# A two-layer cached-attention decode kernel, rewritten around one circular SBUF buffer: K half on TensorE and half on VectorE, contiguous K/V reads, layer 2 run backwards over the last unit kept

## The chip, the cores and the metric

The kernel runs on one core of one Trainium2 chip; the other cores are idle. The metric is the device time of one execution in microseconds (us), lower is better. Of the kernel before there are three timed runs, with a median of 2951.37 us (2937.76 to 2956.49), and one profiled execution, from which every other figure of the kernel before in this document comes.

## The reference

Two layers, each an attention over a cached K and V for one new token (batch 2, 32 heads, 16384 positions, head size 128) and a small mixer MLP. Everything is bf16. Both layers use the same K, V and weights.

```python
def _A_ref(x, k_cache, v_cache, wq, wo):          # x: (2, 1, 576)
    q = (lambda x, *d: x.transpose(*d))((x @ wq).reshape(B, Sq, H, Dh), 0, 2, 1, 3)   # wq: (576, 4096)
    scores = jnp.einsum("bhqd,bhkd->bhqk", q, k_cache) * (Dh ** -0.5)
    p = _softmax(scores, axis=-1)
    o = jnp.einsum("bhqk,bhkd->bhqd", p, v_cache)
    return (lambda x, *d: x.transpose(*d))(o, 0, 2, 1, 3).reshape(B, Sq, H * Dh) @ wo   # wo: (4096, 576)

def _B_ref(x, w1, w2, w3, w4):
    h = _gelu(_layernorm(x, axis=-1) @ w1)
    g0 = jnp.pad(h[:, :, 0*c:1*c], ((0, 0), (1, 0), (0, 0)))[:, :S, :]   # g1, g2, g3 alike, by 1 or 2
    ...
    hs = jnp.concatenate([g0, g1, g2, g3], axis=-1) @ w2
    x1 = x + hs
    h2 = _gelu(_layernorm(x1, axis=-1) @ w3) @ w4; return x1 + h2   # w3: (576, 4608), w4: (4608, 576)

x = x + _A_ref(_layernorm(x, axis=-1), A_k_cache, A_v_cache, A_wq, A_wo)
x = x + _B_ref(_layernorm(x, axis=-1), B_w1, B_w2, B_w3, B_w4)
x = x + _A_ref(_layernorm(x, axis=-1), A_k_cache, A_v_cache, A_wq, A_wo)
x = x + _B_ref(_layernorm(x, axis=-1), B_w1, B_w2, B_w3, B_w4)
```

The sequence has one position, so each shift moves all of h out and hs is a product of zeros with w2. A unit below is one (batch, head) pair: 64 a layer, each with 4.19 MB of K and 4.19 MB of V.

## The kernel before, in words

`Prog` collects closures for each engine, in the order in which they are added; every semaphore wait is written by hand. `attention_core` (L824 on) walks the 64 units of a layer. Each unit's K and V come in two halves of 2 MB (one tile of 128 partitions x 64 rows x 128, a run of 16 KB for each partition, with 32 KB from one partition's run to the next in HBM: `k_src`, `v_src`). K halves rotate through 4 buffers (`kbuf`), V halves through 5 (`vbuf`), weights through 5 slots (`wring`) with a plan of their own. All loads are issued by SP in one order (L1118 to L1126): K of unit u, then V of unit u-1. In front of a K load SP waits until the old half in that buffer has been used: `kfree_waits` waits for PE's transposes (`sem_kfree_pe`) and DVE's dots (`sem_kfree_dv`, which a one-element copy on DVE, L1044, counts up).

K needs its 128-element rows contracted with q. NCP = 6 of a unit's 16 chunks (a chunk is 8 blocks of 128 rows) go through PE: eight transposes into PSUM (L924), a copy to SBUF on ACT (L994, `ktsb`, 4 buffers), eight matmuls with q as the moving column (L949), 2 chunks behind. The other 10 chunks go through DVE (`dve_dots`): q is spread over the partitions with a diagonal and a matmul of ones (L1006, L962, L1015), then K times q in place (L1036) and a sum over each row (L1039): one pair of instructions for 2 chunks in the first half, one for 8 in the second.

The softmax of a unit: DVE takes the maximum over the two kinds of scores (L1052, L1057, L1063), POOL the maximum over the partitions with `partition_all_reduce` (L1072) and the scaling (L1075), ACT the two exponentials (L1086, L1090), and PE the 128 matmuls with V (L978). On ACT the exponentials stand in the same queue as the copies of the next unit's chunks.

Behind the last unit of a layer comes a chain of small steps: the denominators (POOL, L804 and L807), `wo_projection` over 32 heads (L537), the layernorms (`layernorm_T`, each with a POOL all-reduce), `z_projection` with w3 (L696), gelu, `w4_projection`, the product of w1 whose value is never used (`dead_h_projection`, L757), and the q projection of the next layer. Each matmul of these has a weight tile of 128 x 128 and two moving columns. The loads of w2, w3, w4, w1 and wq are issued at the layer's end, each when a slot of `wring` is free.

Of the kernel before, what the change touches and what calls it, by code (L numbers as in the profile page):

```python
# [8 lines left out]
ROP = bass.bass_isa.ReduceOp  # L9
# [6 lines left out]
class Prog:  # L16
    ENGS = ("sync", "scalar", "tensor", "vector", "gpsimd")

    def __init__(self):
        self.ops = {e: [] for e in self.ENGS}  # L20

    def add(self, eng, fn):
        self.ops[eng].append(fn)

    def emit(self, block):
        for e in self.ENGS:
            fns = self.ops[e]
            if not fns:
                continue

            def runner(eng, fns=fns):
                for fn in fns:
                    fn(eng)
            sect = {"sync": block.sync, "scalar": block.scalar, "tensor": block.tensor,
                    "vector": block.vector, "gpsimd": block.gpsimd}[e]
            sect(runner)


class KB:
    def __init__(self, nc, A_x, K, V, wq, wo, w1, w2, w3, w4, out,  # L40
                 NKB=5, NVB=4, NKT=5, NT=4, LEAD=2, NS=2, NP=2, NW=4, ACT_COPY_EVERY=3,
                 PV_AFTER=None, KV_WAIT_WQ=0, WENG="sync", WO_AT=(8, 16, 24, 32), NCP=None):
        self.nc = nc
        self.prog = Prog()
        self.A_x, self.K, self.V = A_x, K, V
        self.wq, self.wo, self.w1, self.w2, self.w3, self.w4 = wq, wo, w1, w2, w3, w4
        self.out = out
        B, Sq, D = A_x.shape
        Bk, H, S, Dh = K.shape
        assert Bk == B and Dh == 128 and Sq == 1  # L50
        self.B, self.D, self.H, self.S = B, D, H, S
        self.F = w3.shape[1]
        assert self.F % 128 == 0 and B <= 32
        assert tuple(wq.shape) == (D, H * 128) and tuple(wo.shape) == (H * 128, D)
        assert tuple(w1.shape) == (D, D) and tuple(w2.shape) == (D, D) and tuple(w4.shape) == (self.F, D)
        self.NL = 2
        self.U = B * H
        self.NB = S // 128
        self.CH = 8
        assert self.NB % self.CH == 0 and S % 128 == 0  # L60
        self.NC = self.NB // self.CH
        self.NPART = 2 if (self.NC % 2 == 0 and self.NC >= 2) else 1
        self.CP = self.NC // self.NPART
        self.BP = self.NB // self.NPART
        self.NCP = self.NC if NCP is None else NCP
        assert 1 <= self.NCP <= self.NC
        self.NKB, self.NVB, self.NKT, self.NT = NKB, NVB, NKT, NT
        self.LEAD, self.NS, self.NP, self.NW = min(LEAD, self.NCP), NS, NP, NW
        self.ACT_COPY_EVERY = ACT_COPY_EVERY
        self.PV_AFTER = PV_AFTER  # L70
        self.KV_WAIT_WQ = KV_WAIT_WQ
        self.WENG = WENG
        self.WO_AT = WO_AT
        self.KT = (D + 127) // 128
        self.klen = [min(128, D - 128 * t) for t in range(self.KT)]
        self.MT = self.F // 128
        self.scale = float(Dh) ** -0.5
        self.WCOLS = max(H * 128, self.F, self.KT * D, 512)
        self.W4G = max(1, min(self.MT, self.WCOLS // D))
        while self.MT % self.W4G:  # L80
            self.W4G -= 1
        self.WOG = max(1, min(H, self.WCOLS // D))
        while H % self.WOG:
            self.WOG -= 1
        assert self.NT == 4 and self.KT <= 5, "output tile groups use banks tps0..3 + mps"
# [1135 lines left out]
```

## Time and profile before

| what | value |
|---|---|
| median of the timed runs | 2951.37 us (2937.76 to 2956.49) |
| span of the profiled execution | 2954.2 us; nothing lies around it |
| read from HBM | 1116.51 MB, 378 GB/s over the span |
| DMA queue of SP | 96520 packets, 92.9% of 16 engines' span |
| DVE, PE, ACT, POOL busy | 79%, 47%, 28%, 3% |
| K and V loads | 512 tiles of 2 MB |
| granted TensorE clock | 0.521 on the mean |

The page lists busy times by engine, then the span in 40 slices with the busy share in tenths and the rate of the loads; the groups of instructions by line carry the mean time of one; the stretches ("windows") give the busy time of each engine, the granted clock, the DMA share and the rate between two times. A DMA share of 1.00 says that all 16 DMA engines had a packet in hand all the time; small excesses over 1 come from packets counted where they started.

### The profile page before, as it was taken

What the parts mean: (1) busy time and instruction counts of PE and PEld (TensorE: products, weight loads), DVE (VectorE), ACT (ScalarE), POOL (GpSimd) and SP (SyncE); (2) the same over time, 40 slices, a digit from 0 to 9 for tenths busy, and PEclk for the clock granted to TensorE, in tenths of its full rate; (3) what the DMA queues carried; (4) which work ended last, traced back from release to release, by engine and by line L of the source; (5) the groups of instructions that cost most, each with busy time, mean ns of one, the idle gap of its engine ahead of it and who ended that gap; (6) DMA issues with size and microseconds to landing.
All of it is one profiled execution on the core that took longest, in us unless ns stands there. A gap on an engine that the chain in (4) does not pass through costs nothing.

```text
span 2954.2 us, 67140 instructions
## 1 busy us (share of the span) xinstructions
PE 1389.2 (47%) x30282; PEld 1337.0 (45%) x30282; DVE 2325.3 (79%) x1554; ACT 841.6 (28%) x1304; POOL 92.8 (3%) x283
## 2 busy tenths in 40 slices
PE   3454544444544445444544444444454454544445
PEld 3444444444544445444544444444454444444445
DVE  5888888788788888888277887887888878888782
ACT  2322322322323223232122232232232322323221
POOL 0000000000000000000000000000000000000000
PEclk7555555555555555555555555555555555555555
DMA  9999999999999999999599999999999999999984
GB/s 393 411 400 398 393 393 378 379 386 403 386 391 386 398 389 387 393 371 395 193 410 401 398 383 397 388 376 395 385 398 394 386 388 394 380 393 390 380 361 154
DMA packets 96804, 1120.82 MB, mean 379 GB/s; under 512 B 8964, under 2 KB 28680, under 8 KB 28680
## 3 DMA queue, kind: packets, MB, share of 16 engines
q1 hardware_dynamic: 96520, 1116.54, 92.9%
q8 instruction: 238, 3.90, 0.5%
q14 instruction: 46, 0.38, 0.0%
HBM read 1116.51 MB, written 0.00 MB: 378 GB/s over the span
## 4 chain that ended last, share of the span: by engine, by line
issue 53%; PE 31%; ACT 6%; DVE 6%; POOL 3%; DMA 1%; POOLq 0%; ACTq 0%; SPq 0%; DVEq 0%
PE ops L978 14%; PE tps L924 11%; PE sps L949 4%; ACT ktsb L994 4%; ACT p_sb L1090 2%; POOL mall_sb L1072 2%; DVE s_dve L1039 1%; POOL bias_sb L1075 1%; DVE m_sb L1052 1%; DVE m_sb L1057 1%; DVE kbuf L1036 1%; DVE m_sb L1063 1%; ACT p_sb L1086 1%; PE tps L537 1%; DMA kbuf<-in_A_k_cache_dram 0%
## 5 line engine op out<-in xcount | busy, mean ns | idle before, releaser
L1039 DVE TENSOR_REDUCE s_dve<-kbuf 128x16 f32<-128x2048 bf16 (+1 forms) x256 | 1404.3, 5486 | 8.8
L949 PE MATMUL sps<-qt_sb,ktsb 128*128 128x1 bf16 x6144 | 302.2, 170 | 1321.9 <-ACT ktsb L994 1320.6
L949 PEld LDWEIGHTS sps<-qt_sb,ktsb 128*128 128x128 bf16 x6144 | 303.3, 114 | 1355.2 <-ACT ktsb L994 1353.7
L994 ACT ACTIVATE ktsb<-tps 128x1024 bf16<-128x1024 bf16 x768 | 741.3, 1023 | 424.7 <-PE tps L924 419.3
L924 PE MATMUL tps<-ident,kbuf 128*128 128x128 bf16 x6144 | 782.3, 309 | 13.5 <-DMA kbuf<-in_A_k_cache_dram 9.0
L1036 DVE TENSOR_TENSOR kbuf<-kbuf,qb_sb 128x2048 bf16<-128x2048 bf16 (+1 forms) x256 | 723.2, 2825 | 12.9 <-issue 1.3
L924 PEld LDWEIGHTS tps<-ident,kbuf 128*128 128x128 bf16 x6144 | 602.4, 140 | 15.1 <-DMA kbuf<-in_A_k_cache_dram 9.3
L1086 ACT ACTIVATE p_sb<-sps,bias_sb 128x48 bf16<-128x48 f32 x128 | 38.4, 300 | 1566.5 <-POOL bias_sb L1075 1566.5
L978 PE MATMUL ops<-p_sb,vbuf 128*128 128x1 bf16 x16384 | 456.0, 165 | 26.6 <-ACT p_sb L1086 19.7
L978 PEld LDWEIGHTS ops<-p_sb,vbuf 128*128 128x128 bf16 x16384 | 447.4, 104 | 26.8 <-ACT p_sb L1086 19.8
L1052 DVE TENSOR_REDUCE m_sb<-s_dve 128x1 f32<-128x80 f32 x128 | 30.2, 236 | 374.2 <-PE sps L949 373.9
L962 PE MATMUL mps<-diag_sb,ones_bf 128*128 128x128 bf16 x128 | 36.9, 289 | 136.4 <-DVE diag_sb L1006 136.4
L1072 POOL PARTITION_ALL_REDUCE mall_sb<-m_sb x128 | 50.3, 393 | 1282.6 <-DVE m_sb L1063 1238.5
L1075 POOL TENSOR_SCALAR bias_sb<-mall_sb 128x1 f32<-128x1 f32 x128 | 35.7, 279 | 1448.3 <-issue 1448.3
L962 PEld LDWEIGHTS mps<-diag_sb,ones_bf 128*128 128x128 bf16 x128 | 13.4, 105 | 146.7 <-DVE diag_sb L1006 146.7
L1015 DVE CAST qb_sb<-mps 128x128 bf16<-128x128 f32 x128 | 37.2, 291 | 53.9 <-PE mps L962 53.9
L1044 DVE CAST junk<-ident 128x1 f32<-128x1 bf16 x256 | 39.4, 154 | 27.1 <-DVE s_dve L1039 0.9
L1090 ACT ACTIVATE p_sb<-s_dve,bias_sb 128x80 bf16<-128x80 f32 x128 | 44.7, 349 | 0.0
L1006 DVE TENSOR_SCALAR diag_sb<-ident,qt_f 128x128 bf16<-128x128 bf16 x128 | 31.6, 247 | 0.1
L354 ACT ACTIVATE rstd<-var,epsb 128x2 f32<-128x2 f32 x8 | 2.4, 295 | 100.9 <-DVE var L347 100.9
L1057 DVE TENSOR_REDUCE m_sb<-sps 128x1 f32<-128x48 f32 x128 | 26.5, 207 | 4.5
L815 DVE RECIPROCAL rden_sb<-den_sb 128x64 f32<-128x64 f32 x2 | 1.1, 552 | 31.9 <-POOL den_sb L807 31.9
(91 smaller groups left out, 282.4 us busy)
## 6 DMA issues: line engine op xcount, KB each, us to landing
kbuf<-in_A_k_cache_dram SPq DMA_DIRECT2D x256, 2048.0 KB, 10.1
vbuf<-in_A_v_cache_dram SPq DMA_DIRECT2D x256, 2048.0 KB, 18.6
wring<-in_B_w_dram SPq DMA_DIRECT2D x12, 864.0 KB, 9.9
wring<-in_A_wo_dram SPq DMA_DIRECT2D x8, 1152.0 KB, 23.0
wring<-in_B_w_dram SPq DMA_DIRECT2D x8, 1152.0 KB, 6.8
wring<-in_A_wq_dram SPq DMA_DIRECT2D x8, 1024.0 KB, 9.8
wring<-in_B_w_dram SPq DMA_DIRECT2D x6, 576.0 KB, 8.6
wring<-in_A_wq_dram SPq DMA_DIRECT2D x2, 512.0 KB, 12.4
```

The lines of the kernel that those rows point to most:

```text
L924: ins = pe.transpose(self.tps[slot][:, i * 128:(i + 1) * 128], self.kbuf[kslot][:, jj, :], self.ident[:, :])
L949: ins = pe.matmul(self.sps[sb][:, j:j + 1], lhsT=self.ktsb[:, ks, i, :], rhs=self.qt_sb[:, gu:gu + 1], start=True, stop=True)
L978: ins = pe.matmul(self.ops_[:, gu:gu + 1], lhsT=self.vbuf[vslot][:, jj, :], rhs=self.p_sb[pb][:, j:j + 1], start=(j == 0), stop=(j == NB - 1))
L994: ins = eng.activation(out=self.ktsb[:, ks, :, :], in_=src, func=ACT.Copy)
L1036: dv.tensor_tensor(out=kap, in0=kap, in1=qb_bc, op=ALU.mult).then_inc(self.sems["sem_dotm"], 1)
L1039: dv.tensor_reduce(out=self.s_dve[ss][:, j0 - NBP:j1 - NBP], in_=kap, axis=AX.X, op=ALU.add).then_inc(self.sems["sem_dot"], 1)
L1052: i1 = dv.tensor_reduce(out=self.m2_sb[:, gu:gu + 1], in_=self.s_dve[sb][:, 0:NBD], axis=AX.X, op=ALU.max)
L1057: i2 = dv.tensor_reduce(out=self.m_sb[:, gu:gu + 1], in_=self.sps[sb][:, 0:NBP], axis=AX.X, op=ALU.max)
L1072: g_.partition_all_reduce(self.mall_sb[:, gu:gu + 1], self.m_sb[:, gu:gu + 1], channels=128, reduce_op=ROP.max).then_inc(self.sems["sem_po ...
L1075: g_.tensor_scalar(out=self.bias_sb[:, gu:gu + 1], in0=self.mall_sb[:, gu:gu + 1], scalar1=-scale, scalar2=None, op0=ALU.mult).then_inc(se ...
L1086: act.activation(out=self.p_sb[pb][:, 0:NBP], in_=self.sps[sb][:, 0:NBP], func=ACT.Exp, bias=self.bias_sb[:, gu:gu + 1], scale=scale, accu ...
L1090: act.activation(out=self.p_sb[pb][:, NBP:NB], in_=self.s_dve[sb][:, 0:NBD], func=ACT.Exp, bias=self.bias_sb[:, gu:gu + 1], scale=scale, a ...
```

## The change

The kernel is written anew; only the mathematics of a chunk stays. The parts are:

- **`Sched`** replaces the hand-written semaphores: every operation names what it reads and writes, and waits are worked out at build time. One counting semaphore an engine, 32 in turn for the DMAs.
- **`Ring`**: one SBUF tensor of 12 slots of 2 MB. All loads (K, V and weights) are queued in order of use and placed one behind another, wrapping at the end. `pump` runs at build time: a load is issued, on SP, as soon as the tiles that lie under its place have been released, and it waits for their last readers. A tile marked `keep` is stepped over.
- **Reads**: half h of a unit's K or V is now 16384/2 consecutive rows, so 2 MB in one piece: partition p holds 64 consecutive rows, and the next partition's run of 16 KB follows directly.
- **K half on PE, half on DVE**: half 0 (8 chunks) is transposed on PE and copied by ACT, half 1 (8 chunks) goes through DVE in pieces of one chunk, into two product buffers instead of in place.
- **Softmax**: the maximum over the partitions comes from an fp32 matmul with a scaled identity (`unit_max`) and a DVE reduction; POOL only makes constants. The query rows come from one matmul of a broadcast q column with the identity, copied by ACT.
- **Order**: the first two chunks of unit i are turned before `unit_max` of unit i-1; its exponentials stand behind the fifth copy on ACT; V of unit i-1 is weighed behind unit i's eight turns.
- **Output projection** in groups of 8 heads (`group_out`), four a layer; layernorm sums over partitions on PE; gelu through Exp, so that one ACT table serves everything.
- **Layer 2 backwards**: unit 63 is last in layer 1 and first in layer 2; its K and V (4 slots) stay in the ring. w2 is loaded once, w1 never.

The diff, cut to its core (the old functions stand above; `pump` belongs to `Ring`, all that follows to `Decode`; behind the loop of `plan` shown here w3 is queued in 5 tiles, w4 in 3, and in layer 1 wq in 5):

```diff
-    k = KB(nc, A_x, A_k_cache, A_v_cache, A_wq, A_wo, B_w1, B_w2, B_w3, B_w4, out, NKB=4, NVB=5, NW=5, NKT=4, NCP=6, ACT_COPY_EVERY=1)
-            return K[b, hh].rearrange("(p j) d -> p j d", p=128)[:, h * BP:(h + 1) * BP, :]
+    CH = 8
+    LEAD = 2
+    NKT = 3
+    NSLOT = 12
+    GH = 8
+    N_KEEP = 1
...
+    def pump(self):
+        while self.queue:
+            key, n, src, aligned = self.queue[0]
+            p = self._place(n, aligned)
+            if p is None:
+                return
+            under = [t for t in self.live if t["off"] < p + n and p < t["off"] + t["n"]]
+            if not all(t["done"] for t in under):
+                return
+            self.queue.pop(0)
+            deps = [o for t in under for o in self.s.readers(t["res"])]
...
+            self.s.dma(lambda e, src=src, view=view: src(e, view), w=[t["res"]], deps=deps)
+        def kv(src, u, h):
+            b, hh = u % B, u // B
+            ap = src[b, hh].rearrange("(t p j) d -> t p (j d)", t=2, p=128)[h]
+            return lambda e, v: e.dma_start(v, ap)
+        self.order = [list(range(self.U)), list(reversed(range(self.U)))]
...
+        want_wq(0)
+        for l in range(2):
...
+            for i, u in enumerate(order):
+                if u not in skip:
+                    for h in range(2):
+                        ring.want(("K", l, u, h), TB * 128, kv(self.K, u, h))
...
+                if i >= 1:
+                    self.want_v(kv, l, i - 1, skip, jrows)
+            self.want_v(kv, l, self.U - 1, skip, jrows)
...
+    def turn(self, l, i, c):
...
+            for j in range(self.CH):
+                ins = pe.transpose(self.tps[b][:, j * 128:(j + 1) * 128],
+                                   kt[:, (j0 + j) * 128:(j0 + j + 1) * 128], self.ident[:, :])
...
+        self.act(lambda a: a.activation(out=self.ktsb[k][:, :, :].rearrange("p a b -> p (a b)"), in_=self.tps[b][:, :],
+                                        func=ACT.Copy), r=[f"P:tps{b}"], w=[f"ktsb{k}"])
...
+    def dots(self, l, i, c):
...
+        self.dve(lambda v: v.tensor_tensor(out=self.prod[d][:, :, :], in0=k3, in1=bcast_mid(self.qb[q][:, :], self.CH),
+                                           op=ALU.mult), r=[res, f"qb{q}"], w=[f"prod{d}"])
+        self.dve(lambda v: v.tensor_reduce(out=self.sd[q][:, o:o + self.CH], in_=self.prod[d][:, :, :], axis=AX.X,
+                                           op=ALU.add), r=[f"prod{d}"], w=[f"sd{q}"])
...
+    def unit_max(self, l, i):
...
+        self.pe(lambda pe: pe.matmul(self.misc[:, 128:256], lhsT=bcast(self.m[:, q:q + 1], 128), rhs=self.identS[:, :],
+                                     start=True, stop=True), r=[f"m{q}", "identS"], w=["P:misc"])
+        self.dve(lambda v: v.tensor_reduce(out=self.bias[:, q:q + 1], in_=self.misc[:, 128:256], axis=AX.X, op=ALU.max,
+                                           negate=True), r=["P:misc"], w=[f"bias{q}"])
+    def attention(self, l):
...
+        for i in range(U):
+            dv = list(range(NCP, NCH))
+            for c in range(NCP):
+                self.turn(l, i, c)
+                if len(self.waiting) > self.LEAD:
+                    self.score()
+                if i >= 1 and c == 1:
+                    self.unit_max(l, i - 1)
+                if i >= 1 and c == 4:
+                    self.exps(l, i - 1)
+                if c >= 1:
+                    for _ in range(-(-len(dv) // (NCP - c))):
+                        self.dots(l, i, dv.pop(0))
+            if i >= 1:
+                self.weigh(l, i - 1, 0)
+            while self.waiting:
+                self.score()
+            if i >= 1:
+                self.weigh(l, i - 1, 1)
+                if i % n == 0:
+                    self.group_out(l, i - 1)
+            if i + 1 < U:
+                self.query_rows(l, i + 1)
+            self.row_max(l, i)
```

**SP, a stretch of units in layer 1.** Each row is one load; the names in brackets are the semaphores on which SP stands before it (before: the frees of the K and V buffers; now: the counters of PE and DVE).

Before:

```order
L898 DMA kbuf<-in_A_k_cache_dram 128x8192 [waits sem_kfree_dv,sem_kfree_pe]
L898 DMA kbuf<-in_A_k_cache_dram 128x8192 [waits sem_kfree_dv]
L905 DMA vbuf<-in_A_v_cache_dram 128x8192 [waits sem_vfree] x2
L898 DMA kbuf<-in_A_k_cache_dram 128x8192 [waits sem_kfree_dv,sem_kfree_pe]
L898 DMA kbuf<-in_A_k_cache_dram 128x8192 [waits sem_kfree_dv]
```

Now:

```order
L296 DMA ring<-in_A_v_cache_dram 128x8192 [waits done_tensor] x2
L296 DMA ring<-in_A_k_cache_dram 128x8192 [waits done_tensor]
L296 DMA ring<-in_A_k_cache_dram 128x8192 [waits done_vector]
L296 DMA ring<-in_A_v_cache_dram 128x8192 [waits done_tensor] x2
L296 DMA ring<-in_A_k_cache_dram 128x8192 [waits done_tensor]
```

The order of the loads is the same. Before, a K load waits for the half that came two units earlier (4 buffers) and a V load for the half five back. Now each load waits for the tile 12 loads back: K of unit i for K of unit i-3, V of unit i-1 for V of unit i-4. The first half is free after PE's transposes alone, the second after DVE's dots alone.

**SP, between the layers.** After the last V tile of layer 1 (the kept unit's own two are the ones that wait for DVE and PE) come the weights and then layer 2, without K or V of unit 63.

```order
L307 DMA ring<-in_A_wo_dram 128x8x576 [waits done_tensor]
L296 DMA ring<-in_A_v_cache_dram 128x8192 [waits done_vector]
L296 DMA ring<-in_A_v_cache_dram 128x8192 [waits done_tensor]
L301 DMA ring<-in_B_w_dram 128x4608 [waits done_tensor] x2
L301 DMA ring<-in_B_w_dram 128x4608
L301 DMA ring<-in_B_w_dram 128x4608 [waits done_vector]
L303 DMA ring<-in_B_w_dram 64x4608
L307 DMA ring<-in_B_w_dram 128x12x576 [waits done_tensor] x3
L301 DMA ring<-in_A_wq_dram 128x4096 [waits done_tensor]
```

By the placement that `pump` makes, w3 and the first two of the three w4 tiles lie on the places of V of unit 60, K of unit 62 and V of unit 61; the last w4 tile and the first two wq tiles on V of unit 62; the third and fourth wq tile behind wo; the fifth on w3. The first K tile of layer 2 (unit 62) lies on w3, the next three on w3 and w4, V of unit 62 on w4 and wq.

**DVE, one unit.** Before (`kbuf` is K in place, `m_sb` the maximum, `qb_sb` the query rows):

```order
L1052 TENSOR_REDUCE m_sb<-s_dve 128x1 [waits sem_dot,sem_scc]
L1057 TENSOR_REDUCE m_sb<-sps 128x1 [waits sem_dve_a]
L1063 TENSOR_TENSOR m_sb<-m_sb 128x1 [waits sem_dve_a]
L1006 TENSOR_SCALAR diag_sb<-ident,qt_f 128x128 [waits sem_qb_pe]
L1015 CAST qb_sb<-mps 128x128 [waits sem_dot,sem_qb_pe]
L1036 TENSOR_TENSOR kbuf<-kbuf,qb_sb 128x2048 [waits sem_exp2,sem_qb_dv,sem_k0]
L1039 TENSOR_REDUCE s_dve<-kbuf 128x16 [waits sem_dotm]
L1044 CAST junk<-ident 128x1 [waits sem_dot,sem_kfree_dv]
L1036 TENSOR_TENSOR kbuf<-kbuf,qb_sb 128x8192 [waits sem_exp2,sem_qb_dv,sem_k1]
L1039 TENSOR_REDUCE s_dve<-kbuf 128x64 [waits sem_dotm]
L1044 CAST junk<-ident 128x1 [waits sem_dot,sem_kfree_dv]
```

Now (`prod` is the product buffer, `bias` the scaled negative maximum; the pair L569, L572 stands eight times in a unit, shown twice):

```order
L580 TENSOR_REDUCE m<-sps 128x1 [waits done_tensor]
L582 TENSOR_REDUCE m<-sd 128x1 [waits done_vector]
L584 TENSOR_TENSOR m<-m 128x1 [waits done_vector]
L592 TENSOR_REDUCE bias<-misc 128x1 [waits done_tensor]
L569 TENSOR_TENSOR prod<-ring,qb 128x1024 [waits dma18]
L572 TENSOR_REDUCE sd<-prod 128x8 [waits done_vector]
L569 TENSOR_TENSOR prod<-ring,qb 128x1024
L572 TENSOR_REDUCE sd<-prod 128x8 [waits done_vector]
```

The query rows have left DVE; the maximum over the partitions has come to it, with one trip to PE and back (L592 waits for PE) between a unit's maximum and the next unit's dots.

1554 lines of the change are left out of this document (503 added, 1051 removed).

## The prediction

> **What bounds the kernel now.** I read the page first, then the rate in stretches, then SP's waits, then one unit on DVE.
>
> ```profile
> span 2954.2 us, 67140 instructions
> ...
> PE 1389.2 (47%) x30282; PEld 1337.0 (45%) x30282; DVE 2325.3 (79%) x1554; ACT 841.6 (28%) x1304; POOL 92.8 (3%) x283
> ...
> DMA  9999999999999999999599999999999999999984
> ...
> q1 hardware_dynamic: 96520, 1116.54, 92.9%
> q8 instruction: 238, 3.90, 0.5%
> ```
>
> The loads fill nearly every slice; no engine does. The stretches tell whether the loads are at their limit (from and to, length, busy time and instructions of PE, PE's weight loads, DVE, ACT and POOL, then granted clock, DMA share, GB/s):
>
> ```profile
> 0.00:4.00 4.00, 0.00 (x0) 0.00 (x0) 0.00 (x0) 1.28 (x1) 0.83 (x14) 1.00 0.42 130
> 4.00:12.00 8.00, 0.00 (x0) 0.00 (x0) 0.00 (x0) 0.00 (x0) 0.00 (x0) 1.00 1.01 411
> 12.00:18.00 6.00, 0.38 (x5) 0.31 (x5) 0.72 (x5) 0.00 (x0) 0.28 (x1) 1.00 1.06 246
> 20.00:60.00 40.00, 17.04 (x369) 16.56 (x370) 32.08 (x27) 13.04 (x18) 2.51 (x3) 0.73 1.01 427
> 60.00:100.00 40.00, 18.61 (x402) 17.65 (x399) 35.56 (x23) 9.06 (x13) 1.02 (x3) 0.50 1.00 421
> ...
> 1000.00:1400.00 400.00, 193.04 (x4229) 186.53 (x4227) 329.53 (x207) 118.48 (x183) 12.11 (x37) 0.51 0.95 388
> 1404.00:1436.00 32.00, 12.82 (x354) 12.29 (x355) 12.23 (x8) 6.40 (x13) 1.95 (x5) 0.50 0.02 4
> 1456.00:1468.00 12.00, 8.36 (x120) 7.45 (x120) 1.22 (x5) 1.55 (x2) 0.00 (x0) 0.50 1.09 357
> ...
> 1600.00:2800.00 1200.00, 562.99 (x12340) 543.58 (x12341) 987.57 (x603) 351.80 (x549) 36.49 (x110) 0.51 0.95 389
> ```
>
> With many loads queued (20 to 100 us) K and V arrive at 427 and 421 GB/s, share 1.00; over whole stretches of units at 388 and 389, share 0.95. At the layer's end next to nothing is loaded for 32 us (4 GB/s). So the bound is the loads, with holes. Who makes the holes stands in SP's queue and in the engines' waits:
>
> ```profile
> SPq L898 <- PE sps L949: 1283.3, 122, 13.5
> SPq L122 <- DVE junk L1044: 880.7, 124, 26.1
> ```
>
> ```profile
> POOL bias_sb L1075 <- issue: 1448.3, 128, 13.8
> ...
> PE sps L949 <- ACT ktsb L994: 1320.6, 126, 13.8
> ```
>
> SP stands before its K loads nearly all the time, for PE's scores and DVE's dots. POOL's scaling comes up to 13.8 us late, the exponentials behind it hold ACT, ACT holds the copies, PE waits 1320.6 us for them, and K buffers come free late. With room for two units of K, the queue then runs empty.
>
> **What the change does, part by part.**
>
> *The queue.* Each load now waits for the tile 12 back, three units instead of two for K, and half 0 no longer depends on DVE, half 1 no longer on PE. If a unit's work takes less than its load, the queue never empties. A unit is 4 x 2.097 = 8.39 MB, at 424 GB/s (between the two full rows) 19.8 us. The work, first DVE:
>
> ```profile
> L1039 DVE TENSOR_REDUCE s_dve<-kbuf 128x64 f32<-128x8192 bf16 x128 | 1111.7, 8685 | 4.4
> ...
> L1036 DVE TENSOR_TENSOR kbuf<-kbuf,qb_sb 128x8192 bf16<-128x8192 bf16 x128 | 566.3, 4424 | 1.3 <-issue 1.3
> ...
> L1039 DVE TENSOR_REDUCE s_dve<-kbuf 128x16 f32<-128x2048 bf16 x128 | 292.6, 2286 | 4.4
> L1036 DVE TENSOR_TENSOR kbuf<-kbuf,qb_sb 128x2048 bf16<-128x2048 bf16 x128 | 156.9, 1226 | 11.6
> ```
>
> ```profile
> 1026.59 0.23 DVE L1052 TENSOR_REDUCE m_sb<-s_dve 128x1 f32<-128x80 f32 x1 [2.77 <-PE sps L949]
> ...
> 1027.11 0.16 DVE L1063 TENSOR_TENSOR m_sb<-m_sb 128x1 f32<-128x1 f32 x1
> 1027.18 0.25 DVE L1006 TENSOR_SCALAR diag_sb<-ident,qt_f 128x128 bf16<-128x128 bf16 x1
> 1027.81 0.29 DVE L1015 CAST qb_sb<-mps 128x128 bf16<-128x128 f32 x1 [0.38 <-PE mps L962]
> 1028.20 1.23 DVE L1036 TENSOR_TENSOR kbuf<-kbuf,qb_sb 128x2048 bf16<-128x2048 bf16 x1
> 1029.46 2.29 DVE L1039 TENSOR_REDUCE s_dve<-kbuf 128x16 f32<-128x2048 bf16 x1
> ```
>
> From the two widths the product costs 0.16 us + 0.52 ns an element, the sum 0.15 us + 1.04 ns. A piece of 1024 is 0.69 + 1.22 us, and 0.03 between dependent ones (1028.20 + 1.23 to 1029.46): 1.97, eight of them 15.8 us, for 16.6 us of dots today (2.29 + 1.23 + 8.69 + 4.42). The maximum takes 0.7 (1026.59 to 1027.27). The trip to PE and back is new: 0.38 idle for a bf16 matmul today; the fp32 matmul has no row. Bounds: 0.38, and 0.38 plus four times the 0.29 us of L962, 1.5; I take 0.8. Then 0.3 for the bias. **DVE's loop is 17.6 us**; with 0.38 it is 17.2, with 1.5 and one more fixed 0.15 us for each of the 16 pieces 20.7.
>
> PE and ACT:
>
> ```profile
> 1043.18 3.41 PE ops L978 x128
> 1046.60 0.88 PE tps L924 x8
> 1047.47 0.19 PE sps L949 x8
> ```
>
> ```profile
> L994 ACT ACTIVATE ktsb<-tps 128x1024 bf16<-128x1024 bf16 x768 | 741.3, 1023 | 424.7 <-PE tps L924 419.3
> ```
>
> PE: 8 x (0.88 + 0.19) + 3.41 + 0.8 for query rows and maximum = 12.8 us. ACT: 8 x 1.02 + 0.3 + 1.0 = 9.5 us. Both lie beside DVE. The one new wait on PE, `unit_max` behind two turns, holds back six turns and the V matmuls: PE then has 12.8 - 2.1 = 10.7 us to do in DVE's 17.6, so it comes back before DVE needs it. Every 16 units PE waits in `group_out` for DVE and DVE for 2.7 us of wo: about 3.5 us, which 2.2 us of spare time a unit make up in two units while up to 8 loads are queued. POOL's delays are gone from the chain.
>
> *The bytes.* 508 tiles of K and V instead of 512 (8.4 MB less); one w2 instead of two, no w1 (2.0 MB less): 1106.1 MB. At the rate of the row that is nearest to each:
> - K, V: 1065.4 MB at 424 GB/s: 2512.7 us. Reads in one piece have no row of 16 KB packets; bounded by 411 (wq's contiguous reads, 4 to 12 us): +80 us, and by 427: -18.
> - wo, w4, w2, rows of 1152 bytes: 20.7 MB at 357 (w4 at 1456): 58.0 us.
> - wq, w3, full height: 17.8 MB at 411: 43.4 us; their last, 64-row tiles: 2.2 MB at 246 (wq's at 12 to 18): 9.1 us.
> - instructions (q8): 257 PE steps a unit for 225, so 4.4 MB: 10.5 us.
> - until the loads run: 4 us less 0.52 MB, 2.8 us.
>
> *Between the layers.* The old rows price the new steps:
>
> ```profile
> 1444.10 0.18 DVE tmpT L318
> ...
> 1446.58 0.18 DVE xb L374
> ...
> 1450.71 5.07 PE sps L696 x180
> 1455.80 0.54 DVE z_f L712
> ...
> 1457.71 0.27 PE tps L537 x4
> 1458.12 0.20 PE tps L537 x4
> 1458.46 0.20 PE tps L537 x4
> ```
>
> A layernorm is 2.7 us, z 5.1, gelu 1.9 (1455.80 to 1457.71), w4 0.34 for each of 36 blocks (1458.12 to 1458.46), wo the same for a head. Count from the arrival of layer 1's last V tile: V 2, normalize 1, wo's last 8 heads 2.7, two layernorms and x1 5.6: 11.3; z to 16.4; gelu 18.3; w4 waits for its own bytes (w3 14 us, w4 15) and ends at 33; layernorm 36; wq is there at 41, q at 42.5. The loads meanwhile: w3 and w4 lie on places that unit 62 has left; wq's fifth tile needs w3's first (free at 12) and is due at 39; the first K tile of layer 2 needs w3's fourth (free at 16) at 41, the third w4's middle (28) at 51, V of unit 62 wq (42) at 61. **No hole**: 0 us for today's 32. Then unit 63 runs without a load, and DVE, freed at 60, works off unit 62, whose first half is needed back at 81. If the loads did stop for the whole chain, it would cost 42 us.
>
> *The end.* The last w4 third lands 29 us after the last V byte, all loads still in a row; then 12 blocks (4.1 us), the add (0.9), cast, turn, copy and store, which begin here and take 3 us to the span's end:
>
> ```profile
> 2951.23 0.10 DVE xo_bf L270
> ```
>
> With 0.3 for the waits between them 8.3 us.
>
> Sum: 2512.7 + 58.0 + 43.4 + 9.1 + 10.5 + 2.8 + 8.3 = **2645 us** against the span of 2954.2, which is 2.8 over the median: **2642 us** on that scale.
>
> As a check, work alone: 155 us outside the unit loops (28 until wq, w2 and the first K are in; 53 between the layers, from the last dots, some 9 us before the last V byte, to the first at 44; 46 at the end, to 37 behind that byte; 8 groups of 3.5) + 128 x 17.6 = 2408. Loads win by some 240 us; DVE would set the time from (2645 - 155) / 128 = 19.5 us a unit.
>
> **The rivals.**
> - *DVE becomes the bound.* Its loop must pass 19.5 us, and my upper bound is 20.7. Price, half way between: 155 + 128 x 20.1 = 2728 us, at worst 2805. For it: small pieces and a trip to PE; against: the 0.03 us gaps today.
> - *The full rate doesn't last.* The rows of 421 to 427 cover 80 us. If 389 at share 0.95 is 409 at full share, K and V take 2605: 2735 us; if 389 itself is the memory's rate, 1106.1 MB take 2843 + 11 = 2854. Against it: the holes have names in SP's queue.
> - *The memory gives contiguous K less, and the kernel is slower.* All engines now read inside one 2 MB piece. It decides from (1065.4 MB in 2951 - 132 us) 378 GB/s down; at 357, the lowest full-height row, 1065.4 MB take 2984 + 132 = 3116 us. For it: 357 is seen, on short rows; against: wq, contiguous, at 411.
> - *The ring doesn't prefetch across the boundary* (the kept tiles stand in the way): 2642 + 42 = 2684 us.
>
> Beside the third: the Trainium skill ("SBUF — State Buffer", Summary: rules for kernel authors) says to reckon with about 358 GB/s from HBM. By that, an estimate from the page, all bytes would take 3090 us, slower than now. Its "HBM Reference" (Specifications) gives a core alone about 425 and the 358 only to two cores that stream together. The rows of 421 and 427 bear out the second page.
>
> **How the numbers follow.** Forecast 0.75, DVE-bound 0.12, the rate doesn't last 0.07, slower 0.03, no prefetch 0.03. The forecast's own range is 2610 to 2690. The range must leave out no more than 0.2: below, 2600 (427 GB/s and a shorter end); above, 2750, which takes in the boundary case, the 411 bound and most of the first two rivals. A change of under 1% can't be told from none. Faster 0.96, same 0.01, slower 0.03.
>
> **What would show it.** DMA share 1.00 and 420 GB/s or more in stretches of units; no hole at half time; SP's waits long but harmless; DVE busy about 2200 us with gaps that wait for K; K's landing far over today's, since the queue is deep. Wrong: shares of 0.95 with DVE busy throughout (first rival), share 1.00 at 390 (second) or under 378 (third).

## The result, and the profile after

The changed kernel takes 2665.22 us (median, 2664.48 to 2665.49), the kernel before 2953.93 us beside it: 0.9037 of its time, 95% interval 0.9012 to 0.9061, or 288.7 us less. The forecast was 2642, range 2600 to 2750. The page of the profiled execution:

```profile
span 2663.4 us, 74240 instructions
...
PE 1558.8 (59%) x34587; PEld 1461.0 (55%) x34587; DVE 1979.6 (74%) x2649; ACT 1098.5 (41%) x1681; POOL 0.8 (0%) x10
...
DMA  9999999999999999999999999999999999999998
...
q1 hardware_dynamic: 94072, 1106.16, 99.0%
q8 instruction: 270, 4.42, 0.7%
```

SP's queue now fills 99.0% of the 16 engines' span instead of 92.9. The slice at half time, 5 before, is now 9, and the last two, 84 before, are 98. The page's table of issues says the same: a half of K lands 46.5 us after its issue (median), 10.1 before, because so many loads stand queued ahead of it. The stretches, a long one, a short one without a load of weights, and those of the two layer ends:

```profile
100.00:1200.00 1100.00, 642.47 (x14283) 600.72 (x14281) 844.61 (x1108) 464.32 (x711) 0.00 (x0) 0.66 1.00 423
474.00:633.00 159.00, 93.26 (x2072) 87.29 (x2072) 122.11 (x160) 67.98 (x103) 0.00 (x0) 0.66 1.01 426
1280.00:1300.00 20.00, 11.26 (x258) 10.44 (x258) 14.25 (x20) 8.15 (x12) 0.00 (x0) 0.67 0.88 354
1300.00:1320.00 20.00, 8.62 (x186) 7.81 (x187) 5.31 (x24) 1.73 (x8) 0.00 (x0) 0.50 1.00 362
1320.00:1340.00 20.00, 8.71 (x300) 8.30 (x297) 1.26 (x4) 0.49 (x2) 0.00 (x0) 0.50 1.02 314
1340.00:1360.00 20.00, 10.39 (x249) 9.86 (x250) 3.26 (x11) 2.22 (x5) 0.00 (x0) 0.50 1.02 363
2600.00:2620.00 20.00, 10.14 (x243) 9.31 (x241) 15.64 (x21) 7.78 (x15) 0.00 (x0) 0.67 0.88 353
```

The first row has share 1.00 and 423 GB/s where whole stretches had 0.95 and 388; between two loads of wo it is 426. At half time the loads go on, though at 314 to 363 GB/s while the weights are read. The waits have turned round:

```profile
PE ops L617 <- DMA ring<-in_A_v_cache_dram: 555.2, 240, 5.4
...
PE tps L539 <- DMA ring<-in_A_k_cache_dram: 336.8, 113, 4.6
...
DVE prod L569 <- DMA ring<-in_A_k_cache_dram: 255.3, 117, 3.7
```

Before, PE stood 1320.6 us for ACT's copies. Now PE and DVE stand for tiles that have not landed.

How fast the loads really are is read from the units. ACT's copy of the query rows comes once a unit; these are the 16th, the 24th and the 32nd:

```profile
310.87 0.28 ACT L526 ACTIVATE qb<-misc 128x128 bf16<-128x128 f32 x1 [6.97 <-PE misc L524]
473.47 0.28 ACT L526 ACTIVATE qb<-misc 128x128 bf16<-128x128 f32 x1 [6.88 <-PE misc L524]
633.14 0.28 ACT L526 ACTIVATE qb<-misc 128x128 bf16<-128x128 f32 x1 [7.33 <-PE misc L524]
```

Eight units take 159.67 us, 19.96 each, or 67.11 MB at 420 GB/s; the eight with a wo load among them take 162.60, so 1.18 MB of wo costs 2.93 us. (Single steps are 19.6 us and, every fourth, 21.1, so a whole number of fours has to be taken. The window over the same time says 426: some 2 of it are the loads of instructions, 4.42 MB over the span; the rest was not traced.)

DVE's loop as it runs when it waits for no load is seen just behind the layers' boundary, where tiles lie ready. The bias of two units in a row, and of a unit in the steady part its first product and the maxima behind its eighth sum:

```profile
1407.16 0.29 DVE L592 TENSOR_REDUCE bias<-misc 128x1 f32<-128x128 f32 x1 [0.89 <-PE misc L590]
1423.61 0.29 DVE L592 TENSOR_REDUCE bias<-misc 128x1 f32<-128x128 f32 x1 [0.89 <-PE misc L590]
```

```profile
1006.71 0.69 DVE L569 TENSOR_TENSOR prod<-ring,qb 128x1024 bf16<-128x1024 bf16 x1 [2.11 <-DMA ring<-in_A_k_cache_dram]
1007.44 1.22 DVE L572 TENSOR_REDUCE sd<-prod 128x8 f32<-128x1024 bf16 x1
1008.58 0.68 DVE L569 TENSOR_TENSOR prod<-ring,qb 128x1024 bf16<-128x1024 bf16 x1
...
1021.54 0.21 DVE L580 TENSOR_REDUCE m<-sps 128x1 f32<-128x64 f32 x1
```

The loop is 16.45 us: dots 14.83 (1006.71 to 1021.54), maxima 0.53, the trip to PE 0.89, the bias 0.29. These sum to 16.54; the rest is overlap, since an instruction can start some 0.08 us before the one ahead ends. The loop is 3.5 us less than a unit's loads need.

### The profile page after: what moved, and what is told of

Same layout as the page of the kernel before. It is cut to its first block, busy times and chain, and to the rows that moved or that the text cites. A ratio compares the mean times of both kernels' runs of the same rounds, so it can differ in the third digit from the quotient of the medians.

```text
span 2663.4 us, 74240 instructions
## 1 busy us (share of the span) xinstructions
PE 1558.8 (59%) x34587; PEld 1461.0 (55%) x34587; DVE 1979.6 (74%) x2649; ACT 1098.5 (41%) x1681; POOL 0.8 (0%) x10
## 3 DMA queue, kind: packets, MB, share of 16 engines
q8 instruction: 270, 4.42, 0.7%
## 4 chain that ended last, share of the span: by engine, by line
DMA 67%; PE 11%; DVE 8%; another core or an unknown queue 8%; ACT 4%; SPq 1%; issue 1%
DMA ring<-in_A_v_cache_dram 35%; DMA ring<-in_A_k_cache_dram 28%; DVE sd L572 5%; PE ops L617 5%; PE tps L539 4%; DMA ring<-in_B_w_dram 4%; ACT ktsb L543 3%; DVE prod L569 3%; PE sps L557 1%; PE misc L590 1%; DMA ring<-in_A_wq_dram 1%; ACT p L603 1%; SPq L301 0%; PE misc L457 0%
## 5 line engine op out<-in xcount | busy, mean ns | idle before, releaser
L572 DVE TENSOR_REDUCE sd<-prod 128x8 f32<-128x1024 bf16 x1024 | 1249.0, 1220 | 35.4
L543 ACT ACTIVATE ktsb<-tps 128x1024 bf16<-128x1024 bf16 x1024 | 992.7, 1028 | 514.6 <-PE tps L539 509.1
L539 PE MATMUL tps<-ident,ring 128*128 128x128 bf16 x8192 | 829.2, 268 | 336.8 <-DMA ring<-in_A_k_cache_dram 336.8
L569 DVE TENSOR_TENSOR prod<-ring,qb 128x1024 bf16<-128x1024 bf16 x1024 | 698.7, 682 | 256.0 <-DMA ring<-in_A_k_cache_dram 255.3
L539 PEld LDWEIGHTS tps<-ident,ring 128*128 128x128 bf16 x8192 | 673.4, 123 | 366.5 <-DMA ring<-in_A_k_cache_dram 358.6
L617 PE MATMUL ops<-p,ring 128*128 128x1 bf16 x16384 | 471.2, 165 | 564.8 <-DMA ring<-in_A_v_cache_dram 555.2
L617 PEld LDWEIGHTS ops<-p,ring 128*128 128x128 bf16 x16384 | 450.1, 102 | 585.8 <-DMA ring<-in_A_v_cache_dram 571.7
L557 PE MATMUL sps<-qt,ktsb 128*128 128x1 bf16 x8192 | 349.9, 166 | 93.4 <-ACT ktsb L543 85.1
L557 PEld LDWEIGHTS sps<-qt,ktsb 128*128 128x128 bf16 x8192 | 313.0, 102 | 132.8 <-ACT ktsb L543 131.6
L592 DVE TENSOR_REDUCE bias<-misc 128x1 f32<-128x128 f32 x128 | 37.3, 291 | 260.6 <-PE misc L590 260.6
L590 PE MATMUL misc<-identS,m 128*128 128x128 f32 x256 | 95.5, 476 | 34.6 <-DVE m L584 34.6
## 6 DMA issues: line engine op xcount, KB each, us to landing
ring<-in_A_k_cache_dram SPq DMA_DIRECT2D x254, 2048.0 KB, 46.5
ring<-in_B_w_dram SPq DMA_DIRECT2D x8, 1152.0 KB, 23.4
```

What stands on the lines that cost most here:

```text
L539: ins = pe.transpose(self.tps[b][:, j * 128:(j + 1) * 128], kt[:, (j0 + j) * 128:(j0 + j + 1) * 128], self.ident[:, :])
L543: self.act(lambda a: a.activation(out=self.ktsb[k][:, :, :].rearrange("p a b -> p (a b)"), in_=self.tps[b][:, :], func=ACT.Copy), r=[f"P:t ...
L557: ins = pe.matmul(self.sps[sp][:, col:col + 1], lhsT=self.ktsb[k][:, j, :], rhs=self.qt[:, u:u + 1], start=True, stop=True)
L569: self.dve(lambda v: v.tensor_tensor(out=self.prod[d][:, :, :], in0=k3, in1=bcast_mid(self.qb[q][:, :], self.CH), op=ALU.mult), r=[res, f" ...
L572: self.dve(lambda v: v.tensor_reduce(out=self.sd[q][:, o:o + self.CH], in_=self.prod[d][:, :, :], axis=AX.X, op=ALU.add), r=[f"prod{d}"], ...
L590: self.pe(lambda pe: pe.matmul(self.misc[:, 128:256], lhsT=bcast(self.m[:, q:q + 1], 128), rhs=self.identS[:, :], start=True, stop=True), ...
```

## The experiments

The experiments test the prediction's theory that the holes came from POOL's late scaling, through ACT and PE to the K buffers. The rivals tested are the depth of the buffers, the layout of the reads, DVE, and the queue. The edits are cut to their core.

**POOL put back into the changed kernel.** In `unit_max`:

```diff
-        self.pe(lambda pe: pe.matmul(self.misc[:, 128:256], lhsT=bcast(self.m[:, q:q + 1], 128), rhs=self.identS[:, :],
-                                     start=True, stop=True), r=[f"m{q}", "identS"], w=["P:misc"])
-        self.dve(lambda v: v.tensor_reduce(out=self.bias[:, q:q + 1], in_=self.misc[:, 128:256], axis=AX.X, op=ALU.max,
-                                           negate=True), r=["P:misc"], w=[f"bias{q}"])
+        self.pool(lambda g: g.partition_all_reduce(self.mall[:, q:q + 1], self.m[:, q:q + 1], channels=128,
+                                                   reduce_op=ROP.max), r=[f"m{q}"], w=[f"mall{q}"])
+        self.pool(lambda g: g.tensor_scalar(out=self.bias[:, q:q + 1], in0=self.mall[:, q:q + 1], scalar1=-self.scale,
+                                            scalar2=None, op0=ALU.mult), r=[f"mall{q}"], w=[f"bias{q}"])
```

> The changed kernel with the old way of the maximum over the partitions: all-reduce and scaling on POOL in place of the fp32 matmul and the reduction on DVE. Theory A (POOL's scaling came 11 us late in the kernel before because DVE was busy in single instructions of 2.3 to 8.7 us; here they are 0.7 and 1.2 us): the wait shrinks to 1 or 2 us and the time stays at 2665 us, within 10. Theory B (POOL is late by itself): the bias comes 11 us late, ACT holds the exponentials and the last three copies back, a unit takes about 21.5 us instead of 19.7, so about 2900 us.

Measured: 2863.82 us (2835.8 to 2874.61), 0.9689 of before (0.9626 to 0.9752): 199 us of the gain are gone, with ring, layout and order as in the change. That is nearer to theory B (2900) than to A (2665). Two stretches, and the waits:

```profile
200.00:600.00 400.00, 213.02 (x4925) 205.92 (x4925) 291.52 (x369) 163.33 (x247) 13.56 (x38) 0.62 1.00 419
...
1500.00:2400.00 900.00, 462.94 (x10608) 447.88 (x10606) 621.84 (x787) 351.15 (x533) 31.77 (x83) 0.62 0.98 397
```

```profile
POOL bias L594 <- issue: 1422.3, 128, 13.5
...
PE sps L559 <- ACT ktsb L545: 1266.2, 131, 14.5
ACT p L605 <- POOL bias L594: 1209.1, 128, 13.6
```

POOL's own work doesn't slow the loads: it has 9.5 instructions in 100 us in the row with 419 GB/s and 9.2 in that with 397. But the rate falls further than the share does (397 at 0.98 here, 389 at 0.95 before, 423 at 1.00 in the change), so a share just under 1 understates the holes; why it does wasn't tested. Two instructions of POOL that follow one another:

```profile
1020.41 0.38 POOL L592 PARTITION_ALL_REDUCE mall<-m  x1 [9.58 <-DVE prod L571]
1032.26 0.26 POOL L594 TENSOR_SCALAR bias<-mall 128x1 f32<-128x1 f32 x1 [11.47 <-issue]
```

The chain of before stands there again: the scaling comes 11.1 us behind the all-reduce (1422.3 / 128; before 1448.3 / 128 = 11.3), ACT waits for it, PE for ACT's copies. DVE's pieces are short here (1.2 us at most) where before they ran up to 8.7, so the delay doesn't come from the length of DVE's instructions.

Nor is an all-reduce slow as such. This is the chain behind the last unit of layer 1 in the kernel before, where DVE waits 15.65 us for POOL and next to nothing is loaded ("issue" is time in which POOL waits for nothing that the profile shows):

```profile
1415.80 0.38 POOL mall_sb L1072
1416.25 7.09 issue
1423.34 0.27 POOL bias_sb L1075
...
1425.07 5.47 issue
1430.54 0.74 POOL den_sb L807
...
1444.50 0.17 DVE stat L323
1444.77 0.46 POOL tot L330
1445.25 0.18 DVE mean L341
```

L1072, L807 and L330 are all-reduces; L1075, and L804 between it and L807, are ordinary instructions. From the one kind to the other POOL lets 7.1 and 5.5 us pass. L330, an all-reduce behind another all-reduce, gives DVE its sum 0.6 us after the last input. Over the whole of before's trace, the scaling comes 7.0 us or more behind the all-reduce in all 128 units, and no gap from an ordinary instruction to an all-reduce is under 5.7 us, though most of these hold a wait for the maximum too. This points to the alternation of the two kinds, twice a unit, and not to the reduction as such. It is read from the trace and not shown by a run: L330 and L807 add, where L1072 takes a maximum, and what POOL does in the gap, and why it is longer in the units than here, the profile doesn't show. With POOL put back, the two gaps take 1422.3 and 1286.6 us in 128 units, 21.2 a unit (by the list of waits only 145.3 us of it are for the maximum): this alone is over the 19.96 us of the loads, so in that run POOL by itself is slower than they are. Leaving the all-reduce on POOL and moving only the scaling elsewhere was not tried.

**The other way round: the kernel before with this one part of the change.** Buffers, loads, order and dots stay; behind DVE's maximum PE spreads the column over the partitions (`m` is the column of `m_sb`), and DVE takes the maximum behind the copy of the query rows:

```diff
-            g_.partition_all_reduce(self.mall_sb[:, gu:gu + 1], self.m_sb[:, gu:gu + 1], channels=128,
-                                    reduce_op=ROP.max).then_inc(self.sems["sem_pool"], 1)
-            self.wt(g_, "sem_pool", gu + 1)
-            g_.tensor_scalar(out=self.bias_sb[:, gu:gu + 1], in0=self.mall_sb[:, gu:gu + 1], scalar1=-scale,
-                             scalar2=None, op0=ALU.mult).then_inc(self.sems["sem_bias"], 1)
+            g_.matmul(self.mps[:, 256:384], lhsT=bass.AP(tensor=m.tensor, offset=m.offset, ap=[list(m.ap[0]), [0, 128]]),
+                      rhs=self.identS[:, :], start=True, stop=True).then_inc(self.sems["sem_pool"], 1)
+        def dve_bias(dv, ul):
+            self.wt(dv, "sem_pool", gu + 1)
+            dv.tensor_reduce(out=self.bias_sb[:, gu:gu + 1], in_=self.mps[:, 256:384], axis=AX.X, op=ALU.max,
+                             negate=True).then_inc(self.sems["sem_bias"], 1)
...
-            self.pool(lambda gp_, uu=uu: pool_allreduce(gp_, uu))
+            self.pe(lambda gp_, uu=uu: pool_allreduce(gp_, uu))
```

> The kernel before with one part of the change alone: the maximum over the partitions is taken by a PE matmul with the scaled identity and a DVE maximum instead of POOL's all-reduce and scaling. Buffers, loads, order and dots stay. Theory A (POOL's 11 us a unit made ACT late, and this made the K buffers late): the exponentials come about 9 us earlier in each unit, the loads run at 420 to 424 instead of 391 GB/s in 2500 us of steady stretch: 2950 - 195 = 2755 us. Theory B (the short supply of buffers and the two kinds of buffer hold the rate too): at full share the loads of before ran at 407 GB/s, so 2950 - 100 = 2850 us. Theory C (POOL is only where the wait is seen, not its cause): 2930 us or more. In A the gap between the layers (239 GB/s for 100 us) and the end stay.

Measured: 2717.68 us (2715.98 to 2718.42), 0.9223 of before (0.9208 to 0.9238). One maximum in another place takes off 230.4 us, four fifths of what the whole rewrite takes off. Stretches, and two waits:

```profile
200.00:1200.00 1000.00, 544.17 (x11318) 525.93 (x11318) 901.81 (x600) 323.38 (x498) 0.00 (x0) 0.55 1.01 425
...
1300.00:1400.00 100.00, 55.82 (x1107) 51.86 (x1107) 38.91 (x95) 22.14 (x32) 2.78 (x6) 0.53 0.86 318
```

```profile
SPq L906 <- DVE junk L1052: 1476.9, 119, 13.3
SPq L122 <- DVE junk L1052: 642.9, 117, 26.2
```

425 GB/s at share 1.01, with the old four K buffers: theory A. SP stands before its K loads nearly as long as before (2217.7 us with 97.9 for PE's scores, against 2494.7), and nothing is lost by it, since enough loads are already queued (a half of K lands 23.9 us after its issue, 10.1 before). More came than the 195 us of the steady stretches that I had reckoned with: the boundary gained too, 318 GB/s in its worst 100 us where before has 239. The granted TensorE clock, 0.653 on the mean in the change, can't be the cause: here it is 0.55 in the full stretch, close to the 0.521 of before.

**The layout.** First the changed kernel with the old pitch of 32 KB between partitions:

```diff
-            ap = src[b, hh].rearrange("(t p j) d -> t p (j d)", t=2, p=128)[h]
+            ap = src[b, hh].rearrange("(p j) d -> p (j d)", p=128)[:, h * TB * 128:(h + 1) * TB * 128]
```

> The changed kernel with the old reads: each half of a unit's K or V is again 128 runs of 16 KB with 32 KB from one to the next; all else as changed. Queue theory (the gain is that the load queue no longer runs empty): the rate in stretches of units stays at 426 GB/s and the time at 2665 us, within 10. Layout rival (reads in one piece are what lifted the rate from 389 to 426): K and V fall back to 389 GB/s, 1065.4 MB take 2739 instead of 2501 us, so about 2900 us.

Measured: 2663.5 us (2662.86 to 2664.48): no difference, as the queue theory has it. Then the kernel before with reads in one piece alone (K, and V alike):

```diff
-            return K[b, hh].rearrange("(p j) d -> p j d", p=128)[:, h * BP:(h + 1) * BP, :]
+            return K[b, hh].rearrange("(t p j) d -> t p j d", t=2, p=128)[h]
```

> The kernel before with the new reads alone: each half of K or V is 2 MB in one piece. Queue theory: no change, 2945 to 2960 us, DMA share 0.95 and 388 to 391 GB/s in stretches of units. Layout rival: the rate rises towards 426, so 2720 to 2760 us.

Measured: 2936.25 against 2946.55 us, 0.9963 (0.9941 to 0.9985): some 10 us where there are holes, 9 us under the range that I had set, and nothing where the queue is full. The layout rival wanted some 200.

**Bytes and depth.** No unit kept; then 9 and 6 places instead of 12 as well:

```diff
-    N_KEEP = 1
+    N_KEEP = 0
-    NSLOT = 12
+    NSLOT = 9
```

> The changed kernel with no unit kept: layer 2, still backwards, loads K and V of unit 63 again, 8.39 MB more. Byte theory (the loads are the bound, so each byte costs its time at 426 GB/s): 2665 + 19.7 = 2685 us; a few us less if the four places that are no longer held let the loads run on between the layers, where 14.6 us are lost now. Rival (the kept tiles matter only for the order between the layers): under 5 us of difference.

> As the run without a kept unit, with a ring of 9 places of 2 MB in all (the kernel before had 4 for K, 5 for V and others for the weights) instead of 12. Release theory (what fills the queue is that tiles are given back soon after they arrive; K's second half, the slowest, is held about 17 us, under 5 loads of 4.9 us): no change against the run without a kept unit in stretches of units, 426 GB/s; between the layers, where the weights fill 7.8 places, up to 20 us more: 2685 to 2705 us. Depth rival (12 places are what keeps the queue full): with 9 the share falls below 1 in stretches of units and the time rises by more than 50 us, to over 2735 us.

> As the run without a kept unit, with a ring of 6 places of 2 MB. Release theory: K's second half, held longest, is given back some 13 us after it lands, its place is wanted again 24 us after (5 loads); so 423 GB/s or more still hold in stretches of units, and only the stretch between the layers (weights of 7.8 places) and the end get longer, by at most the 42 us of the chain of small steps: 2685 to 2730 us. Depth rival: the rate in stretches of units falls under 400 GB/s, over 2800 us.

Measured: 2684.47, 2684.32 and 2683.88 us. The 8.4 MB cost 19.3 us, their time at the units' pace. Fewer places cost nothing down to six, one and a half units, which still read 423 GB/s in stretches of units. The "three units instead of two" of the change gained nothing.

**DVE's room.** Sums of 1.22 us whose result nobody reads, behind the maximum of each unit, one of them and then (`range(4)`) four:

```diff
+        for x in range(1):
+            self.dve(lambda v, x=x: v.tensor_reduce(out=self.junk[:, x, :], in_=self.prod[1][:, :, :], axis=AX.X, op=ALU.add),
+                     r=["prod1"], w=[f"junk{x}"])
```

> The changed kernel with one more sum over 1024 elements on DVE in each unit (1.22 us; its result isn't used). DVE's loop is 17.5 us, the loads' 19.7. Load theory: no change, 2665 us within 5, the longer loop lies in DVE's wait for K. Rival (DVE's loop sets the time): 128 x 1.22 = 156 us more, 2821 us.

> The same with four more sums a unit, 4.9 us: DVE's loop 22.4 us is over the loads' 19.7. Load theory with the limit where the prediction put it (19.5 us a unit): 155 + 128 x 22.4 = 3022 us, DVE share near 1 in stretches of units, DMA share under 0.95. If the limit lies higher, less than 2950 us.

Measured: 2666.21 with one, as expected, and 2674.96 with four, where I expected 3022. A unit with four:

```profile
1030.40 0.22 DVE L581 TENSOR_REDUCE m<-sps 128x1 f32<-128x64 f32 x1
...
1030.86 4.59 DVE L588 TENSOR_REDUCE junk<-prod 128x8 f32<-128x1024 bf16 x4
1035.36 0.28 DVE L596 TENSOR_REDUCE bias<-misc 128x1 f32<-128x128 f32 x1
...
1050.38 0.21 DVE L581 TENSOR_REDUCE m<-sps 128x1 f32<-128x64 f32 x1
```

The loop is 20.0 us (1030.40 to 1050.38): 16.45 and 4.59, less the 0.89 of the trip to PE that the sums hide and small overlaps. I had added their full price to the 17.5 us of a steady unit, which contain waits for the load. At 20.0 us the two limits meet: PE now waits 823.6 us for DVE's maximum and hardly for a tile of K or V, while the loads still run at 423 GB/s from 1500 to 2400 us. The price is only 10 us. A loop clearly longer than the loads' was not run.

**wo's rows on another queue.** SP around one wo load of the changed kernel (start and length of the issue):

```profile
294.79 4.24 SPq L307 DMA_DIRECT2D ring<-in_A_wo_dram  x1
299.07 37.78 SPq L296 DMA_DIRECT2D ring<-in_A_v_cache_dram  x2
```

Behind wo (1024 rows of 1152 B) SP needs 37.78 us for two issues, where one takes some 4 us in the steady stretch, and the 100 us around it read 420 GB/s instead of 426. So the loads of wo, then (`("wo", "w3", "w4")`) those of w3 and w4 too, were issued by ACT:

```diff
+            eng = "scalar" if key[0] in ("wo",) else "sync"
-            self.s.dma(lambda e, src=src, view=view: src(e, view), w=[t["res"]], deps=deps)
+            self.s.dma(lambda e, src=src, view=view: src(e, view), w=[t["res"]], deps=deps, eng=eng)
```

> The changed kernel with the wo loads alone (1024 rows of 1152 B each) issued by ACT instead of SP; tiles, order and waits are as they were. Theory A: each dip of about 2.7 us behind a wo load in the middle of a layer comes from the one queue, where the next V load is issued 31 to 42 us late because wo's 1024 rows fill it: with two queues SP's issues are back at 4 us, the dips go, and six of them give 16 us: 2649 us. Theory B: the dips are what rows of 1152 B cost on any queue: no change, 2663 to 2667 us. A third outcome: the issue holds ACT as it held SP, for 30 us, and the loop of the units stands still behind it: 2700 us or more.

> As the run before, and the loads of w3 and w4 between the layers and at the end are issued by ACT too. Theory A (one queue, filled by small rows): the 14.6 us lost between the layers shrink as well, since the next K and V loads run beside w4: 2638 to 2645 us. Theory B (small rows and loads of 64 partitions cost this much on any queue): 2649 us as the run before, or 2663 to 2667 if that one moved nothing.

Measured: 2665.07 (2663.21 to 2667.2) and 2703.47 us (2702.08 to 2705.62). The first moved nothing, as theory B has it, though its dips are gone (425 to 426 GB/s in every 100 us from 100 to 1200). Its units keep the same pace, here the 16th, 24th and 32nd, 322.25 us for 16 where the change takes 322.27:

```profile
312.01 0.28 ACT L527 ACTIVATE qb<-misc 128x128 bf16<-128x128 f32 x1 [8.38 <-PE misc L525]
473.06 0.28 ACT L527 ACTIVATE qb<-misc 128x128 bf16<-128x128 f32 x1 [6.89 <-PE misc L525]
634.26 0.28 ACT L527 ACTIVATE qb<-misc 128x128 bf16<-128x128 f32 x1 [8.15 <-PE misc L525]
```

```profile
1300.00:1320.00 20.00, 10.34 (x244) 9.42 (x244) 7.14 (x22) 1.23 (x6) 0.00 (x0) 0.50 0.58 234
```

The bytes that run ahead are given back in a hole at half time (234 GB/s, 362 in the change). So wo's 2.93 us look like the price of its bytes (2.81 us at the units' 420 GB/s) rather than a stall of the queue. The second run fits neither theory: the issue held the engine that issued.

```profile
1282.01 40.13 ACTq L308 DMA_DIRECT2D ring<-in_B_w_dram  x2
1322.47 0.28 ACT L527 ACTIVATE qb<-misc 128x128 bf16<-128x128 f32 x1 [50.68 <-issue]
```

ACT stood 40 us on two w4 loads, its next copy came after 50.68 us without work, and the layer's last units waited. The same happens at the end of layer 2 (40.74 us), and 38 us are lost in all. That outcome I had named for the run before, where it didn't come: there each of the 8 issues of wo took ACT 0.4 us.

**Two units kept.** If bytes are all, keeping another should give 20 us more:

```diff
-    N_KEEP = 1
+    N_KEEP = 2
```

> The changed kernel with the last two units of layer 1 kept for layer 2 instead of one: 8.4 MB less to read, and of the 12 places of the ring four are left between the layers instead of eight. Theory A (bytes set the time and the depth of the ring doesn't: one kept unit was worth 19.3 us, and 6 places did as well as 12): another 19 to 20 us less, 2645 us. Theory B (with four places left, w3, w4 and wq fill them and the loads of layer 2 start later): the gap between the layers, 14.6 us so far, grows by about as much as is saved, 2660 to 2670 us.

Measured: 2664.92 us (2663.97 to 2666.63), no gain, as theory B has it. Behind the boundary:

```profile
1340.75 13.38 SPq L296 DMA_DIRECT2D ring<-in_A_k_cache_dram  x4
1392.34 0.81 SPq L296 DMA_DIRECT2D ring<-in_A_v_cache_dram  x2
```

```profile
1360.00:1400.00 40.00, 26.11 (x566) 25.00 (x563) 37.47 (x49) 20.18 (x30) 0.00 (x0) 0.67 0.44 177
```

With eight of twelve places held by kept tiles, SP issues four K loads and then nothing until 1392.34; 40 us at 177 GB/s lose 23 us, what the saved bytes had brought. So depth does count once it falls to four places between the layers, where six were enough.

## Why the prediction was right, and where it was off

- **The cause of the holes** was named rightly: POOL's scaling, late by 11 us, holds ACT, ACT holds PE, PE the K buffers. Put back it costs 199 us; taken alone out of the kernel before it brings 230. Why POOL is late the prediction left open; the traces point to its change between two kinds of instruction. The step "with room for two units of K, the queue then runs empty" is half wrong: the chain empties it, but room for two units (before's own buffers) and even the ring's six places keep it full once the chain is short. The depth and the layout of the reads, which make up most of the rewrite's text, bring next to nothing.
- The Trainium skill ("GPSIMD Engine Reference", 4. When to use GPSIMD) gives reductions over partitions to GpSimd. In the units the traces speak against it: 11 us there with the scaling behind it, 0.89 + 0.29 us by way of PE and DVE. In before's layernorm, where all-reduces stand alone, they don't: 0.6 us.
- **What else the rewrite brings**: 52 us between the kernel before with the new maximum and the change. 19.3 are the kept unit. By the rates in the stretches, the gap at half time is some 16 us smaller (318 and 404 GB/s in two times 100 us, now 378 and 411), the end some 20; neither was tried alone. The 2.0 MB of w1 and w2 that aren't read are some 5. Some 10 go back in the steady stretches (423 for 425 GB/s). These make some 50; apart from the kept unit they are estimates from the rates.
- **DVE's loop**: forecast 17.6, measured 16.45. The trip to PE was right (0.8 against 0.89). The dots were 14.8 instead of 15.8: a product, which with two product buffers doesn't depend on the sum ahead of it, starts 0.08 us before that sum ends (1007.44 + 1.22 to 1008.58), where I put a gap of 0.03. (A row of before shown there has it already: L1006 starts at 1027.18, while L1063 ends at 1027.11 + 0.16.) So DVE is busy 1979.6 us, not 2200.
- **The DVE-bound rival** has its place rightly: it decides from about 20 us a unit (forecast 19.5). Its price was too high: 155 us outside the loops is some 115 by the run with four sums (2675 - 128 x 20.0).
- **The sum** was 2645 against a span of 2663.4, 18.4 short. K, V and instructions: 127 units at 19.96 are 2534.9 us, forecast 2512.7 + 10.5: 11.7 too little. With the instructions taken in, the forecast is 422 GB/s, from two rows of 40 us, where the long run gives 420. wo: 8 x 2.93 = 23.4 instead of 26.4 (9.44 MB at 357). What is left, weights, start, boundary and end, is 105.1 instead of 95.4. This remainder is the step **"No hole: 0 us"** and the small tiles, sized too low: there are short holes at both layer ends (share 0.88 in two rows above), and between the layers the loads go at 314 to 363 GB/s with the share full.
- **The prefetch across the boundary** works, as forecast, with one kept unit; with two the rival "the kept tiles stand in the way" is what happens.
- **The memory's rate**: contiguous reads get no less, so the slower case has no ground here. The rival "the full rate doesn't last" has none either: 423 GB/s hold over 1100 us. The Trainium skill's "HBM Reference" (Specifications) gives a core alone about 425 GB/s, and 420 to 426 here agrees; the 358 of its "SBUF — State Buffer" (Summary: rules for kernel authors) does not hold for this core alone.

**Open**: in the run with wo on ACT's queue the windows show more bytes moved by the same time, and the units are no faster. Why a unit's tiles land no earlier was not shown. The Trainium skill ("DMA: Bandwidth & Descriptors", Why a DMA increments its semaphore by 16 and not by 1) says that only the full count, from all engines, means that a load has landed; one engine behind the others would fit. No run here shows the engines apart.

## What to carry to other kernels

When loads have holes, follow the waits back from the queue to the first instruction that is late by itself, and change that alone before buffers or layout: here one maximum of 128 numbers held 230 of 289 us. Look, too, whether the late instruction is late everywhere: an all-reduce was quick where it followed another. Price a load-bound kernel by the pace of its units over a long stretch, and check the stages between the stretches apart. Fewer bytes or a second queue help only where the next limit isn't already there: the second kept unit gained nothing, and of the two runs with loads on ACT's queue one gained nothing and one lost 38 us.

## What the runs showed of the hardware that was not expected

- Behind a load of wo (1024 rows of 1152 B) SP stands for 34 to 43 us on its next two issues. ACT stood 40.13 us on two loads of w4 in a row, though only 0.4 us on a load of wo: an issue isn't always free for an engine that also computes.
- POOL's all-reduce over 128 x 1 shows 0.38 us busy, but the scaling behind it on POOL comes 11 us later, with DVE instructions of 8.7 us beside it as with those of 1.2. In before's layernorms, where an all-reduce follows another, DVE has its result after 0.6 us; from an all-reduce to an ordinary instruction or back, before's trace has no gap under 5.7 us.
- A DMA share near 1 doesn't yet say that the loads run at full rate: 397 GB/s at 0.98, 423 at 1.00.
- A DVE instruction starts 0.07 to 0.09 us before the one ahead ends, where it doesn't need its result, and 0.03 or 0.04 after, where it does.
